# One batch's convolution moved from TensorE to VectorE, its buffers cut into four units, and a new order of work

## The chip, the cores and the metric

The kernel runs on one core of one Trainium2 chip. The time is the device time of one execution, in microseconds (us); a profiled execution also gives the span from its first to its last instruction. The engines are TensorE (PE in the profile; its weight loads are PEld), VectorE (DVE), ScalarE (ACT), GpSimd (POOL) and SyncE (SP). GpSimd issues nearly all loads, SyncE the stores and some transposes by DMA.

## The reference

An attention without softmax, whose normed result goes through a feed-forward layer with a gate made by a convolution over the sequence. B = 8 batches, H = 8 heads, S = 576 positions, D = 64; the model is 512 wide and the hidden layer 1024.

```python
kv = np.einsum('bhsd,bhse->bhde', k, v)
out = np.einsum('bhsd,bhde->bhse', q, kv)
rms = np.sqrt(np.mean(out * out, axis=-1, keepdims=True) + 1e-06)
attn = out / rms * g_norm
x = attn.transpose(0, 2, 1, 3).reshape(B, S, H * D)
h = np.maximum(x @ w_in, 0.0)
hp = pad(h, one position on either side)
conv_out = sum(conv_w[k][None, None, :] * hp[:, k:k + S, :] for k in range(3))
gate = 1.0 / (1.0 + np.exp(-conv_out))
return h * gate @ w_out
```

## The kernel before

The work is cut into small operations, each a Python function marked `@op`. A long string, `ORDER` (L67 to L121), lists them as tokens: `hm.1.7@4` calls `hm(1, 7)` and gives it PSUM bank 4 (or a slot of a ring of buffers), `:1` picks VectorE in place of ScalarE for a copy or a relu (for `qc` and `qc0` the other way round). The loop at L797 runs the tokens, and L807 to L815 chain the instructions of each engine in that order. So every engine runs its own instructions strictly in the order of the list, and the engines meet only where one needs the result, or the buffer, of another.

The steps of a batch b:

- `Lq`, `Lk`, `Lv` (L304 to L310) load q, k and v of a batch through POOL's queue, casting to bf16; each has a ring of two buffers. `Li` and `Lo` load quarters of w_in and halves of w_out. Batch 0 is loaded in pieces by `pre` (L217), batch 1 in halves.
- `kv` (L349) makes the k-v product of a batch on TensorE, `kvc`, `kvn` and `ky` copy it out of PSUM.
- `qt`, `qtp` (L404) turn q round on TensorE and `qc` copies it. For batches 5, 6 and 7 `dq` (L434) does it by a transposing DMA on SP's queue.
- `ot` or `oq` multiplies q with kv, `sq` squares the result. For batches 0 and 1 `on` sums the squares on TensorE, `nl` makes the root on ScalarE and `mu0` the normed x on VectorE. For later batches `oc` copies the result out, `ss` sums the squares, `ln` and `sl` make the factors, `sp` spreads them and `mu` multiplies; batch 7 takes its factors through DRAM (`fw`, `fr`).
- `hm(b, f)` (L634) is one eighth f of the hidden layer: 8 matmuls of 288 columns. `re` is its relu from PSUM into `h`. Batch 1's first two are split into `ha` and `hb`.
- The convolution works on pairs j of eighths. `CONV` groups the batches: group 0 is batch 0, group 1 batch 1, groups 2, 3 and 4 are two batches each. `ta` (L694) writes the two outer taps times h, `aa` (L704) adds them shifted, `ab` adds h, all on VectorE; `sg` (L736) is the sigmoid on ScalarE, which works in the same buffer; `mg` (L748) multiplies h by it on VectorE. In place of `ta`, `aa` and `ab`, `cm(c, f)` (L724) makes the convolution as 6 matmuls with diagonal weights (built by `dg`), and `sg` reads PSUM. The kernel before does that for eighths 6 and 7 of batches 0 and 1.
- `om` (L756) multiplies 128 rows of h by w_out, `ea` copies the result to a row buffer, and `st` stores it through SP. Pairs of batches 0 and 3 (`SPLIT`) take the eight parts in two halves.
- `unread` issues matmuls on a constant whose result nobody reads ("fills").

The convolution's buffers are two tiles, `taps[0]` and `taps[1]` (L198), each for two batches. A group of one batch takes a whole one and uses half of it.

Of the kernel before, what the change touches and what calls it, by code (L numbers as in the profile page):

```python
# [67 lines left out]
pre@0,0,0 unread.10@0 qt0.0.0@0 ps pn pi ca.k.0 ca.v.0 kv.0.0.1@1 kvc.0.0.1.0:1@0 ct@2 qt0.0.1@3 qc0.0.0:1@0
kvc.0.0.1.1 ot.0.0@0 qc0.0.1:1 unread.3@4 kv.0.1.1@3 Lq.1.0@1 pg sq.0.0@0 on.0.0@4 al.x0@0 al.h1@0 nl.0.0@0 pc
dg.7:1 kvc.0.1.1.0:1 dg.6:1 unread.1@6 qt0.0.2@2 kvc.0.1.1.1:1 ot.0.1@6 unread.3@3 kv.0.2.1@3 sq.0.1@1 mu0.0.0  # L70
al.x1@1 Li.1 al.h0@1 kvc.0.2.1.0:1 Li.3 qc0.0.2:1@1 kvc.0.2.1.1:1 on.0.1@4 nl.0.1@1 qt0.0.3@2 Lv.1.0@1 ot.0.2@0
mu0.0.1 sq.0.2@2 qc0.0.3:1 unread.3@3 kv.0.3.1@4,5 kvc.0.3.1.0 on.0.2@6 kvc.0.3.1.1:1 nl.0.2@2 ot.0.3@4 mu0.0.2
sqh.0.3.0@3 unread.3@3 onh.0.3.0@6 sqh.0.3.1 onh.0.3.1 nlh.0.3.0@3 muh.0.3.0 Lk.1.0@1 qt.1.0@0 nlh.0.3.1 qc.1.0:1@2
muh.0.3.1 Li.0 hm.0.2@6 re.0.2 ta.0.2@0 hm.0.3@4 re.0.3 hm.0.6@6 Lq.1.2 ta.0.3 Lv.1.2 re.0.6 aa.0.1 hm.0.7@4 Lk.1.2
Lq.2.0@0 cm.0.6@6 re.0.7:1 sg.0.6@1 kv.1.0.2@0 cm.0.7@4 kvc.1.0.2.0:1@1 kvc.1.0.2.1 sg.0.7 ot.1.0@0 hm.0.1@6 ab.0.1
sq.1.0@4 re.0.1 qt.1.1@4 hm.0.0@2 on.1.0@6 mg.0.3 qc.1.1@3 ot.1.1@4 nl.1.0@4 re.0.0:1 sq.1.1@5 kv.1.2.2@2
kvc.1.2.2.0 ta.0.0@1 mu0.1.0 kvc.1.2.2.1 on.1.1@6 Li.2 ot.1.2@2 nl.1.1@5 ot.1.3@0 ta.0.1 sq.1.2@6 mu0.1.1 aa.0.0
unread.1@6 on.1.2@6 sq.1.3@7 ab.0.0 nl.1.2@6 mu0.1.2 on.1.3@4 nl.1.3@7 Lk.2.0@0 qt.2.0@6 sg.0.3 qt.2.1@4 mu0.1.3
ha.1.2@2 hb.1.2 qc.2.1@4 sg.0.2 qc.2.0@0 ha.1.3@0 hb.1.3 re.1.2 re.1.3 hm.1.7@4 Lv.2.0@0 hm.0.4@2 mg.0.1 Lq.3.0@1
hm.0.5@0 sg.0.1 Lk.3.0@1 Lv.3.0@1 re.1.7 sg.0.0 pl ta.1.2@0 re.0.4 ta.1.3 re.0.5 hm.1.4@4 kv.2.0.4@2 Lo.0 aa.1.1  # L80
ab.1.1 mg.0.0 sg.1.3 sg.1.2 kvc.2.0.4.0@0 hm.1.5@0 kvc.2.0.4.1 ta.0.4@1 ta.0.5 ot.2.0@2 mg.1.1 aa.0.2 hm.1.6@6
re.1.4 ot.2.2@4 re.1.5 sq.2.0@0 ta.1.4@0 ab.0.2 re.1.6 qt.3.1@0 oc.2.0:1@0 qt.3.0@6 qc.3.1@1 hm.1.1@2 ot.2.1@0
sq.2.2@1 sg.0.4 oc.2.2@1 sg.0.5 sq.2.1@2 Lo.1 Lq.4.0@0 Lq.5.0@1 qc.3.0@2 ta.1.5 ot.2.3@4 re.1.1:1 sq.2.3@3 hm.1.0@6
oc.2.1 Lk.4.0@0 Lv.4.0@0 kv.3.0.4@2 re.1.0 ss.2@3 oc.2.3 mg.0.2 ln.8@0 aa.1.2 kvc.3.0.4.0:1@1 kvc.3.0.4.1:1 ab.1.2
unread.3@0 ot.3.0@4 ta.1.0@1 ot.3.1@6 sq.3.0@4 ot.3.2@0 ta.1.1 al.x2@0 oc.3.0@2 aa.1.0 sq.3.2@5 oc.3.2@3 sq.3.1@6
om.0.3.0@2 om.0.0.0@3 oc.3.1 sl.8@0 om.0.1.0@4 ot.3.3@0 om.0.1.4 ab.1.0 om.0.3.4 sq.3.3@7 oc.3.3 sp.2.1@6,0 ss.3@5
dq.5.0@3 ea.0.1@0 mu.2.1.0 Lk.5.0@1 mu.2.1.1 om.0.0.4 ea.0.3@1 ln.1@0 sp.2.0@4,6 mu.2.0.1 mu.2.0.0 dq.5.1@0
om.0.2.0@2 Lv.5.0@1 sg.1.5 sg.1.4 qtp.4.0@0 cm.1.6@6 qc.4.0@4 mg.1.2 ea.0.0@2 hm.2.5@4 sl.1@0 hm.2.2@0 sg.1.1
om.0.2.4 re.2.5 sg.1.6@0 re.2.2 ea.0.2@3 sg.1.0 sp.3.0@6,4 cm.1.7@0 mu.3.0.1 mu.3.0.0 hm.2.4@2 hm.2.7@6 sg.1.7
sp.3.1@0,4 mg.1.0 re.2.4 mg.1.3 kv.4.0.4@2 mu.3.1.0 mu.3.1.1 re.2.7 kvn.4.0.4 ky.4.0.4.0 ky.4.0.4.1 qtp.4.1@6  # L90
hm.3.4@0 hm.3.5@4 re.3.4 oq.4.1@0 re.3.5 qc.4.1@2 ta.2.4@1 ta.2.5 oq.4.0@2 hm.2.6@6 sq.4.0@0 hm.3.3@4 oc.4.0@1
hm.3.6@2 sq.4.1@1 re.2.6 aa.2.2 Lq.7.0@0 hm.3.7@6 re.3.3 oc.4.1 hm.3.1@0 re.3.6 re.3.7 hm.3.2@6 hm.2.3@2 om.0.6.0@4
st.0.0 ab.2.2 ta.2.6@0 sg.2.5 re.3.1 re.3.2 ta.2.7 oq.4.3@6 oq.4.2@0 sg.2.4 re.2.3 kv.5.0.4@5 sq.4.2@2 Lv.7.0@0
Lk.7.0@0 om.0.6.4 om.0.5.0@2 aa.2.3 ab.2.3 Lk.6.0@1 Lv.6.0@1 kvn.5.0.4 sq.4.3@3 oc.4.2@0 mg.2.2 ky.5.0.4.0:1
ea.0.6@4 ss.4@3 dq.7.0@1 oc.4.3 ky.5.0.4.1:1 oq.5.0@0 oq.5.1@4 sq.5.0@4 ta.2.2@1 om.0.5.4 sq.5.1@5 oc.5.0:1@2
om.0.4.0@6 oc.5.1 ta.2.3 oq.5.3@0 oq.5.2@4 aa.2.1 om.0.8.0@7 ea.0.5@5 ab.2.1 sq.5.3@6 om.0.4.4 sq.5.2@7 ss.5 ln.2@0
om.0.8.4 hm.2.1@2 oc.5.2@3 ea.0.8@6 oc.5.3 re.2.1 sl.2@0 hm.2.0@4 sp.4.1@0,2 ea.0.4@7 om.0.7.0@7 re.2.0 mu.4.1.0
mu.4.1.1 sp.4.0@4,0 kv.7.0.4@6 mu.4.0.0 sg.2.2 mu.4.0.1 om.0.7.4 kvn.7.0.4:1 sg.2.3 ea.0.7@2 sp.5.0@4,2 hm.3.0@0
al.h2@1 re.3.0 kx.7.0.4.0 dq.7.1@4 mu.5.0.1 mu.5.0.0 hm.4.5@2 re.4.5 sp.5.1@6,4 hm.4.1@0 mg.2.1 mu.5.1.0 hm.4.2@2
mu.5.1.1 ta.2.0@1 sg.2.7 hm.4.0@6 hm.5.3@4 ta.2.1 re.4.1 sg.2.6 mg.2.3 kx.7.0.4.1 re.4.0 re.4.2 oq.7.0@0 re.5.3  # L100
kv.6.0.4@6 oq.7.1@4 sq.7.0@0 hm.5.2@2 oc.7.0@1 aa.2.0 Lq.6.0@1 hm.4.3@0 st.0.4 dq.6.0@2 sq.7.1@1 oc.7.1 re.5.2
hm.4.4@4 st.0.5 kvn.6.0.4:1 ab.2.0 ta.3.2@0 re.4.3 hm.5.6@0 st.0.1 ta.3.3 hm.5.4@2 hm.5.1@6 sg.2.1 sg.2.0 re.4.4
re.5.6 re.5.1 re.5.4 hm.5.0@4 oq.7.3@6 oq.7.2@0 aa.3.1 re.5.0 mg.2.0 om.1.6.0@2 om.1.3.0@3 ab.3.1 st.0.3 kx.6.0.4.0
st.0.6 ta.3.0@1 dq.6.1@3 sq.7.3@2 sq.7.2@3 ta.3.1 sg.3.3 sg.3.2 hm.5.5@4 oc.7.2@0 st.0.7 aa.3.0 ss.7@0 mg.3.1 ln.4@0
al.x3@1 ab.3.0 ta.3.4@0 ea.1.3@7 re.5.5 om.1.1.0@1 oc.7.3 ea.1.6@5 kx.6.0.4.1 om.1.0.0@0 fw.4 fr.7.0@0 ea.1.1@0
oq.6.0@2 oq.6.2@6 oq.6.3@4 om.1.8.0@1 ta.3.5 ea.1.0@1 sq.6.2@4 fr.7.1@1 oc.6.2@2 oq.6.1@6 aa.3.2 om.1.4.0@0 sq.6.0@5
sq.6.3@6 sq.6.1@7 oc.6.0@3 ss.6@2 ab.3.2 oc.6.1 ea.1.8@4 ln.3@0 ea.1.4@2 hm.4.6@6 om.1.5.0@2 oc.6.3 sl.3@0 st.1.0
mu.7.0.0 sp.6.0@4,0 mu.7.0.1 re.4.6 sg.3.5 sg.3.4 ea.1.5@1 mu.6.0.0 mu.6.0.1 om.1.2.0@6 hm.4.7@4 hm.5.7@0 mu.7.1.0
om.1.7.0@7 re.4.7 sg.3.1 re.5.7 st.0.8 sp.6.1@4,2 st.0.2 st.1.8 mg.3.2 mu.7.1.1 al.h3@0 ta.3.6@0 ea.1.2@6 ea.1.7@3
hm.7.6@0 ta.3.7 sg.3.0 hm.7.2@6 re.7.6 re.7.2 mu.6.1.0 mu.6.1.1 aa.3.3 mg.3.0 ab.3.3 hm.6.0@4 re.6.0 hm.7.1@0  # L110
hm.7.0@4 re.7.1 re.7.0 st.1.2 hm.6.1@0 hm.7.3@4 hm.6.2@6 hm.7.5@2 re.6.1 ta.4.0@1 st.1.1 st.1.7 sg.3.6 sg.3.7 ta.4.1
re.7.3 re.6.2 re.7.5 hm.6.6@0 hm.6.3@4 re.6.6 re.6.3 hm.6.7@2 aa.4.0 mg.3.3 ab.4.0 hm.6.4@4 hm.7.4@0 ta.4.2@0 re.6.7
sg.4.1 sg.4.0 ta.4.3 aa.4.1 om.2.5.0@2 hm.6.5@6 mg.4.0 re.7.4 re.6.4 re.6.5 om.2.7.0@3 hm.7.7@6 ea.2.5@4 ab.4.1
sg.4.2 sg.4.3 re.7.7 ea.2.7@6 ta.4.4@1 om.2.1.0@2 om.2.4.0@6 ta.4.5 aa.4.2 mg.4.1 ab.4.2 ta.4.6@0 ta.4.7 om.3.6.0@3
om.2.2.0@7 ea.2.1@0 st.2.7 st.2.1 aa.4.3 om.2.3.0@2 om.2.8.0@4 om.2.6.0@5 st.1.3 ea.2.4@3 om.3.3.0@6 st.1.5 ab.4.3
om.2.0.0@0 sg.4.4 sg.4.5 ea.2.2@6 ea.2.3@0 sg.4.7 sg.4.6 mg.4.2 mg.4.3 om.3.3.4 ea.2.8@7 ea.2.6@1 om.3.1.0@2
om.3.6.4 st.1.6 om.3.4.0@7 st.2.8 om.3.1.4 om.3.4.4 ea.2.0@5 ea.3.3@7 st.2.2 om.3.2.0@6 oh.3.8.0@0 om.3.5.0@5
# [7 lines left out]
def kernel(  # L125
# [567 lines left out]
    @op  # L693
    def ta(c, f):  # L694
        h, n = span(c)
        if f % 2 == 0:
# [2 lines left out]
        nc.vector.tensor_scalar_mul(tap[:, 0, f % 2, :n, 8:8 + S], h[:, f], cwn[:, 0, f:f + 1])  # L699
        nc.vector.tensor_scalar_mul(tap[:, 1, f % 2, :n, :S], h[:, f], cwn[:, 2, f:f + 1])  # L700
# [145 lines left out]
```

## Time and profile before

| | |
|---|---|
| median of 3 runs | 179.97 us (179.6 to 180.15) |
| span of the profiled execution | 177.6 us |
| `hm` matmuls (L640) | 496 recorded, 64.5 us |
| `om` matmuls (L761) | 268 recorded, 63.0 us |
| `cm` matmuls (L731) | 24, 5.4 us |
| relu on ScalarE (L646) | 61, 37.9 us |
| row copies on ScalarE (L341, 512 wide) | 35, 20.6 us |

A group's line of the profile names the line of code, engine, operation, the tile written and the tiles read, the shape, and a count; then the busy time, the mean of one in ns, and how long its engine sat idle just before such instructions, and for what. Instructions of one engine overlap a little, so the step from start to start is shorter than the mean of one. L341 and L343 are the helper `copy`, and serve many operations.

The chain is read in order of time: start, length, and what the time was spent on. The landing of a load is counted from its issue.

### The profile page before, as it was taken

Reading aid. Unit: us, or ns where it says so; the run is one execution under the profiler, and the core shown is the slowest. Engines: PE = TensorE matmul, PEld = TensorE weight load, DVE = VectorE, ACT = ScalarE, POOL = GpSimd, SP = SyncE. Lnnn points to the kernel's source line nnn. Section 1 sums busy time; section 2 is a strip of 40 time slices with the busy share of each in tenths; the row PEclk is TensorE's granted clock in tenths of the full one; section 3 lists DMA queues with packets and bytes.
Section 4 is the critical chain, followed back from the end, with each engine's and each line's share of the span. In section 5 each row is a group of like instructions: output and inputs, shape, how many; then the busy total and the mean of one; then the engine's idle time right before and its main releaser. Section 6 shows DMA issues by size and latency. Waiting matters only on the chain.

```text
span 177.6 us, 4060 instructions
## 1 busy us (share of the span) xinstructions
PE 168.4 (95%) x1641; PEld 101.3 (57%) x1660; DVE 139.5 (79%) x235; ACT 149.7 (84%) x233; POOL 30.8 (17%) x54
## 2 busy tenths in 40 slices
...
GB/s 155 188 183 197 200 204 201 205 203 206 205 204 203 198 192 139 174 203 198 160 201 179 293 128 0 53 219 263 21 160 0 4 0 143 152 82 99 258 352 219
DMA packets 36219, 29.49 MB, mean 166 GB/s; under 512 B 8528, under 2 KB 31720, under 8 KB 36200
## 3 DMA queue, kind: packets, MB, share of 16 engines
...
q8 instruction: 13, 0.21, 0.4%
...
q10 hardware_dynamic: 40, 0.01, 0.0%
...
## 4 chain that ended last, share of the span: by engine, by line
PE 70%; DMA 20%; POOL 4%; ACT 2%; issue 2%; POOLq 0%; ACTq 0%
PE bank L761 33%; PE bank L640 27%; DMA v_sb<-in_v_dram 10%; DMA k_sb<-in_k_dram 7%; DMA q_sb<-in_q_dram 4%; PE bank L358 3%; PE bank L464 2%; POOL q_sb L241 1%; PE bank L603 1%; PE bank L575 1%; POOL v_sb L241 1%; POOL k_sb L241 1%; PE bank L776 1%; PE bank L731 1%; PE bank L388 1%
## 5 line engine op out<-in xcount | busy, mean ns | idle before, releaser
L640 PE MATMUL bank<-xT,w_in_sb 128*128 128x288 bf16 x496 | 64.5, 286 | 0.1
L761 PE MATMUL bank<-w_out_sb,h 128*128 128x512 bf16 x268 | 63.0, 379 | 1.1 <-issue 0.6
L640 PEld LDWEIGHTS <-w_in_sb 128*128 128x128 bf16 x496 | 47.6, 98 | 14.1 <-issue 0.5
L761 PEld LDWEIGHTS <-h 128*128 128x128 bf16 x280 | 26.3, 98 | 30.6 <-issue 1.9
L646 ACT ACTIVATE h<-bank 128x576 bf16<-128x576 f32 x61 | 37.9, 657 | 4.2 <-PE bank L640 3.9
L745 ACT ACTIVATE taps<-taps,cwn 128x1152 bf16<-128x1152 bf16 (+1 forms) x36 | 38.2, 1094 | 0.1
L341 ACT ACTIVATE row<-bank 128x512 f32<-128x512 f32 (+1 forms) x37 | 21.3, 598 | 12.3 <-PE bank L761 9.3
L751 DVE TENSOR_TENSOR h<-h,taps 128x2304 bf16<-128x2304 bf16 (+1 forms) x20 | 22.2, 1113 | 2.0 <-ACT taps L745 1.2
L706 DVE TENSOR_TENSOR taps<-taps 128x2304 bf16<-128x2304 bf16 (+1 forms) x18 | 20.9, 1160 | 0.4
L712 DVE TENSOR_TENSOR taps<-taps,h 128x2304 bf16<-128x2304 bf16 (+1 forms) x18 | 20.8, 1153 | 0.3
L699 DVE TENSOR_SCALAR taps<-h,cwn 128x1152 bf16<-128x1152 bf16 (+1 forms) x36 | 16.7, 463 | 2.5 <-ACT h L646 2.4
L493 ACT ACTIVATE sq<-bank 128x576 bf16<-128x576 f32 x28 | 17.9, 676 | 0.0
L700 DVE TENSOR_SCALAR taps<-h,cwn 128x1152 bf16<-128x1152 bf16 (+1 forms) x36 | 17.5, 487 | 0.0
L629 DVE SCALAR_TENSOR_TENSOR xT<-o,cw,bank 128x576 bf16<-128x576 f32 x20 | 15.3, 809 | 2.7 <-PE bank L603 2.5
L341 ACT ACTIVATE o<-bank 128x576 f32<-128x576 f32 x22 | 15.0, 694 | 0.0
...
L427 PE MATMUL bank<-fill 128*128 128x512 bf16 x25 | 9.0, 480 | 1.7 <-DVE fill L228 1.5
L358 PEld LDWEIGHTS <-k_sb 96*64 96x64 bf16 x384 | 7.3, 114 | 4.0 <-issue 2.6
L358 PE MATMUL bank<-v_sb,k_sb 96*64 96x64 bf16 x384 | 8.5, 199 | 1.0 <-DMA k_sb<-in_k_dram 0.7
L301 POOL DMA_DIRECT2D k_sb<-in_k_dram x8 | 6.1, 758 | 14.4 <-PE bank L358 12.5
L562 DVE SCALAR_TENSOR_TENSOR xT<-bank,cw,root 128x576 bf16<-128x576 f32 x7 | 5.6, 815 | 1.8 <-ACT root L542 1.7
...
## 6 DMA issues: line engine op xcount, KB each, us to landing
...
q_sb<-in_q_dram POOLq DMA_DIRECT2D x6, 576.0 KB, 13.7
k_sb<-in_k_dram POOLq DMA_DIRECT2D x6, 576.0 KB, 14.7
v_sb<-in_v_dram POOLq DMA_DIRECT2D x6, 576.0 KB, 16.3
...
```

The costliest lines, as they stand in the source:

```text
L341: nc.scalar.activation(to, fr, AX.Copy)
L358: nc.tensor.matmul(ps[i][i * D:(i + 1) * D, t - t0, :], k_sb[:, 2 * t + i, r * D:(r + 1) * D], v_sb[:, 2 * t + i, r * D:(r + 1) * D], star ...
L493: nc.scalar.activation(in_order(b, s), product(b, t), AX.Square)
L640: nc.tensor.matmul(ps[:, e, :HS], w_in_sb[:, t, f * P:(f + 1) * P], x[:, t, e * HS:(e + 1) * HS], start=(t == 0), stop=(t == NT - 1))
L646: nc.scalar.activation(to, fr, AX.Relu)
L699: nc.vector.tensor_scalar_mul(tap[:, 0, f % 2, :n, 8:8 + S], h[:, f], cwn[:, 0, f:f + 1])
L700: nc.vector.tensor_scalar_mul(tap[:, 1, f % 2, :n, :S], h[:, f], cwn[:, 2, f:f + 1])
L706: nc.vector.tensor_add(tap[:, 1, :, :n, :S], tap[:, 0, :, :n, 7:7 + S], tap[:, 1, :, :n, 1:1 + S])
L712: nc.vector.tensor_add(y, y, h[:, 2 * j:2 * j + 2])
L745: nc.scalar.activation(y, y, AX.Sigmoid, scale=cwn[:, 1, f:f + 1])
L751: nc.vector.tensor_mul(h, h, T["tap", c, j][:, 1, :, :n, :S])
L761: nc.tensor.matmul(T["om", p, m], h[:, f, m * P:(m + 1) * P], w_out_sb[:, f, :], start=(f == 0), stop=(f == NF - 1))
```

## The change

Three things. Batch 1's eighths 6 and 7 go the way of the others: `cm.1.6` and `cm.1.7` are gone, `ta.1.6`, `ta.1.7`, `aa.1.3` and `ab.1.3` are new. The two `taps` tiles become one tile of four one-batch units; a new helper `units(n)` takes one or two of them, and a group of one batch now takes one unit. And `ORDER` is replaced throughout: another sequence, other banks and slots, other choices between ScalarE and VectorE, another order of the loads on POOL, of the transposes and stores on SP, and four fills fewer. Behind `pi` the line numbers of the new kernel are 2 higher.

```diff
+    def units(n):
+        s = slots.pop(0)
+        return taps[:, s:s + n].rearrange("p b k f w -> p k f b w")
...
-    taps = [consts.tile([P, 2, 2, 2, TW], BF16, name=f"taps{i}") for i in range(2)]
+    taps = consts.tile([P, 4, 2, 2, TW], BF16, name="taps")
...
-        for t in taps:
-            nc.vector.memset(t[:, 0, :, :, 7:8], 0.0)
-            nc.vector.memset(t[:, 1, :, :, S:S + 1], 0.0)
+        nc.vector.memset(taps[:, :, 0, :, 7:8], 0.0)
+        nc.vector.memset(taps[:, :, 1, :, S:S + 1], 0.0)
...
     def ta(c, f):
...
-            T["tap", c, f // 2] = taps[slots.pop(0)]
+            T["tap", c, f // 2] = units(CONV[c][1])
...
     def sg(c, f):
...
-                T["tap", c, f // 2] = taps[slots.pop(0)]
+                T["tap", c, f // 2] = units(CONV[c][1])
```

Of the order, the stretch from batch 1's last kv to batch 3's kv, before:

```
kv.1.2.2@2
kvc.1.2.2.0 ta.0.0@1 mu0.1.0 kvc.1.2.2.1 on.1.1@6 Li.2 ot.1.2@2 nl.1.1@5 ot.1.3@0 ta.0.1 sq.1.2@6 mu0.1.1 aa.0.0
unread.1@6 on.1.2@6 sq.1.3@7 ab.0.0 nl.1.2@6 mu0.1.2 on.1.3@4 nl.1.3@7 Lk.2.0@0 qt.2.0@6 sg.0.3 qt.2.1@4 mu0.1.3
ha.1.2@2 hb.1.2 qc.2.1@4 sg.0.2 qc.2.0@0 ha.1.3@0 hb.1.3 re.1.2 re.1.3 hm.1.7@4 Lv.2.0@0 hm.0.4@2 mg.0.1 Lq.3.0@1
hm.0.5@0 sg.0.1 Lk.3.0@1 Lv.3.0@1 re.1.7 sg.0.0 pl ta.1.2@0 re.0.4 ta.1.3 re.0.5 hm.1.4@4 kv.2.0.4@2 Lo.0 aa.1.1
...
```

and after:

```
kv.1.2.2@4
ab.0.1 on.1.1@6 kvc.1.2.2.0 kvc.1.2.2.1 ot.1.2@4 nl.1.1@1 ot.1.3@0 mu0.1.1 sq.1.2@0 on.1.2@6 Lq.2.0@0 sq.1.3@1
ta.0.0@2 on.1.3@2 nl.1.2@0 ta.0.1 mu0.1.2 nl.1.3@1 sg.0.2 mu0.1.3 aa.0.0 ab.0.0 ha.1.2@6 ha.1.3@2 mg.0.3 hb.1.2 hb.1.3
re.1.2 ta.1.2@3 hm.0.4@0 kv.2.0.4@4 re.1.3 ta.1.3 qt.2.0@2 sg.0.3 sg.0.0 qt.2.1@6 re.0.4 hm.0.5@0 mg.0.1 aa.1.1 sg.0.1
ta.0.4@0 ab.1.1 mg.0.0 kvc.2.0.4.0@0 kvc.2.0.4.1 sg.1.3 re.0.5 qc.2.1@0 hm.1.6@4 ot.2.2@6 sg.1.2 re.1.6 sq.2.2@0
...
```

The loads on POOL behind batch 0's, in the order of issue (i2 is a quarter of w_in, o0 a half of w_out, q1a a half of batch 1):

```
before: q1a i1 i3 v1a k1a i0 q1b v1b k1b q2 i2 k2 v2 q3 k3 v3 o0 o1 q4 q5 k4 v4 k5 v5 q7 v7 k7 k6 v6 q6
after:  q1a i1 i3 k1a v1a q1b i0 v1b k1b v2 i2 k2 q2 q3 v3 k3 o0 o1 v4 q4 q5 k4 k5 v5 v6 v7 k6 k7 q7 q6
```

The transposes on SP: before `dq.5.0 dq.5.1 dq.7.0 dq.7.1 dq.6.0 dq.6.1`, after `dq.5.1 dq.5.0 dq.7.0 dq.6.1 dq.7.1 dq.6.0`. The two `kx.7` copies, which stood before and behind `dq.7.1`, now follow `dq.6.1`. `st.1.1` moves from among the first stores of its pair to the last stores of the kernel.

More of the change, by code (lines that the diff above doesn't have):

```diff
@@ L67 @@
 ORDER = """
[L68 to L117, printed above, removed]
@@ L118 @@
-om.3.0.0@4 st.2.3 ea.3.6@6 ea.3.1@0 st.3.6 st.3.3 st.3.1 st.2.4 st.2.5 om.3.5.4 om.3.2.4 om.3.7.0@2 st.2.6 ea.3.4@6
-st.2.0 eh.3.8.0@7 st.3.4 om.3.0.4 ea.3.5@0 om.3.7.4 oh.3.8.1 ea.3.2@3 ea.3.0@4 ea.3.7@1 st.3.5 st.1.4 sh.3.8.0
-st.3.2 st.3.0 st.3.7 eh.3.8.1 sh.3.8.1
+pre@0,0,0 al.x0@0 unread.10@6 qt0.0.0@0 pi ct@1 ca.v.0 ca.k.0 qt0.0.1@2 kv.0.0.1@3 kvc.0.0.1.0:1@0 Lq.1.0@1
+qc0.0.0:1@0 kvc.0.0.1.1:1 pg unread.2@6 ot.0.0@4 dg.6:1 kv.0.1.1@3 kvc.0.1.1.1:1 kvc.0.1.1.0:1 sq.0.0@0 Li.1 al.h1@0
+unread.2@6 on.0.0@0 qc0.0.1:1 ot.0.1@6 nl.0.0@0 qt0.0.2@2 pc mu0.0.0 sq.0.1@0 qc0.0.2@0 unread.2@3 kv.0.2.1@3
@@ new lines @@
+kvc.0.2.1.0 on.0.1@0 kvc.0.2.1.1:1 Li.3 nl.0.1@0 Lk.1.0@1 mu0.0.1 unread.1@5 qt0.0.3@4 Lv.1.0@1 ot.0.2@2 sq.0.2@0
+qc0.0.3 unread.3@1 kv.0.3.1@5,0 al.h0@1 kvc.0.3.1.1 Lq.1.2 kvc.0.3.1.0:1 on.0.2@6 ps Li.0 ot.0.3@4 Lv.1.2 nl.0.2@0
+sqh.0.3.0@0 unread.3@0 onh.0.3.0@0 pn sqh.0.3.1 Lk.1.2 mu0.0.2 nlh.0.3.0@1 muh.0.3.0 onh.0.3.1 nlh.0.3.1 qt.1.0@6
+muh.0.3.1 qc.1.0:1@0 Lv.2.0@0 hm.0.2@2 hm.0.6@0 dg.7:1 hm.0.7@4 Li.2 re.0.6 cm.0.6@6 re.0.2 kv.1.0.2@0 sg.0.6@0
+kvc.1.0.2.0@0 kvc.1.0.2.1 re.0.7:1 Lk.2.0@0 hm.0.3@2 cm.0.7@4 ta.0.2@1 ot.1.0@0 qt.1.1@6 sg.0.7 re.0.3:1 sq.1.0@0
```

40 lines of the change are left out of this document (added).

## The prediction

> **What bounds the kernel now.** I read the page first (busy shares, then the chain that ended last), then the busy time by stage, then the chain in order of time, and last where single loads land.
>
> ```profile
> span 177.6 us, 4060 instructions
> PE 168.4 (95%) x1641; PEld 101.3 (57%) x1660; DVE 139.5 (79%) x235; ACT 149.7 (84%) x233; POOL 30.8 (17%) x54
> PE 70%; DMA 20%; POOL 4%; ACT 2%; issue 2%; POOLq 0%; ACTq 0%
> ```
>
> 70% of the chain is TensorE work, and the DMA fifth is loads of q, k and v that TensorE waits for early on. The stages, cut at TensorE's waits, the fifth a part of the fourth (columns: stretch, length, then busy us of PE, PEld, DVE, ACT, POOL, the granted clock, DMA share, GB/s):
>
> ```profile
> 0.00:27.00 27.00, 23.99 (x271) 13.77 (x274) 17.30 (x57) 18.81 (x30) 17.25 (x29) 1.00 1.20 188
> 27.00:36.60 9.60, 8.36 (x120) 6.10 (x121) 9.24 (x18) 9.27 (x16) 4.81 (x14) 1.00 1.33 202
> 36.60:45.90 9.30, 8.90 (x147) 6.46 (x147) 9.18 (x19) 9.26 (x18) 2.38 (x3) 1.00 1.30 205
> 45.90:158.90 113.00, 111.92 (x1030) 67.48 (x1042) 103.73 (x145) 106.27 (x161) 6.38 (x8) 1.00 0.78 143
> 63.90:118.50 54.60, 53.97 (x603) 33.05 (x605) 49.89 (x67) 53.26 (x85) 4.74 (x6) 1.00 1.00 162
> 158.90:177.60 18.70, 15.25 (x78) 7.51 (x77) 0.00 (x0) 6.12 (x11) 0.00 (x0) 1.00 0.65 239
> ```
>
> Until 46 us the DMA engines never rest (about 200 GB/s in every stretch), so a load's landing is set by how many bytes stand ahead of it in POOL's queue, not by when it is issued. From 45.9 TensorE is busy 111.92 of 113 us: there the order of its own work is the time, with ScalarE (106.27) and VectorE (103.73) close behind. The clock is 1.00 throughout. Two pieces of the chain and two landings carry the sum below:
>
> ```profile
> 28.67 17.11 DMA v_sb<-in_v_dram
> 45.91 0.95 PE bank L358 x48
> 47.22 0.32 PE bank L427
> 47.59 0.38 PE bank L427
> 57.05 0.74 PE bank L731 x6
> 60.85 0.85 PE bank L731 x6
> ```
>
> The first two lines: batch 3's v lands at 45.78 and its kv follows at once. The next two are three fill matmuls (an `unread.3`) on the chain. The last two are the convolution matmuls `cm.1.6` and `cm.1.7`.
>
> ```profile
> q_sb<-in_q_dram POOLq DMA_DIRECT2D x1, 576.0 KB, 12.5
> v_sb<-in_v_dram POOLq DMA_DIRECT2D x1, 576.0 KB, 15.6
> ```
>
> These are batch 2's q (issued at 17.07, landed 29.6) and v (issued at 21.03, landed 36.6), the first and the last of the group q, w_in quarter, k, v.
>
> **The change part by part.**
>
> *Off TensorE.* `cm.1.6` and `cm.1.7` go: 0.74 + 0.85 = 1.59 us of the chain. The `unread.3` at 47.2 goes: 0.32 + 0.38 = 0.70. Before 27 us there are 23 fills in both orders, and the single one at 29.0 stood in a wait of the norms: nothing. Gain: 2.29 us, all of it after 36.6.
>
> *Onto VectorE.* `ta.1.6`, `ta.1.7`, `aa.1.3`, `ab.1.3` from these rows (mean ns of one):
>
> ```profile
> L700 DVE TENSOR_SCALAR taps<-h,cwn 128x576 bf16<-128x576 bf16 x12 | 4.8, 398 | 0.0
> L706 DVE TENSOR_TENSOR taps<-taps 128x1152 bf16<-128x1152 bf16 x6 | 4.5, 757 | 0.1
> L712 DVE TENSOR_TENSOR taps<-taps,h 128x1152 bf16<-128x1152 bf16 x6 | 4.5, 753 | 0.1
> L699 DVE TENSOR_SCALAR taps<-h,cwn 128x576 bf16<-128x576 bf16 x12 | 4.4, 364 | 1.6 <-ACT h L646 1.6
> ```
>
> 2 x (0.364 + 0.398) + 0.757 + 0.753 = 3.0 us. The two sigmoids read the buffer (L745, 0.78) and no longer PSUM (L742, 0.65): +0.3 us for ScalarE. The new order also turns engines over: 10 more relus net and 13 output copies go from ScalarE to VectorE, at about 0.66 and 0.61 us from start to start. Added up over the order, ScalarE loses about 9.6 us and VectorE gains about 16.4, of which 1.7 come before 45.9, 3.6 after the last convolution product, and 11.1 between.
>
> *The order of the loads.* Batch 2 was q, w_in, k, v and becomes v, w_in, k, q: the same bytes, so the last place lands at 36.6 as before, but it is now q's. TensorE's list: `kv.1.2.2` (its k lands at 27.0 in both), the norms of batch 1, `ha`/`hb`, `hm.0.4`, `kv.2.0.4`, then `qt.2.0`, which needs that q. The norms end as before (the `mu0.1.3` product at about 32.1, one product earlier in VectorE's list), `hb.1.3` at 32.9, `hm.0.4` 0.98 (L640, 16 matmuls in 1.96), kv 0.88: TensorE stands at 34.7 and q comes at 36.6, a wait of 1.9. `hm.0.5`, which could fill it, is behind `qt.2.0` in the list. Nothing overtakes on TensorE, and what is queued behind (all of batch 1's remaining `hm`) is late with it. Measured as work: by 36.6 the kernel before has done 1.27 (`qt.2`) and 2.57 of `hm` where the new one has done 0.98 + 0.88. It is 1.98 us behind. Bounds: 0 if q lands by 34.7, which the queue's 2.9 us per load (590 KB at 200 GB/s) excludes unless v, w_in or k is smaller; 2.5 if its semaphore is late.
>
> So of 2.29 us saved, 1.98 are spent at 36.6: -0.3.
>
> *The transposes of batch 5.* `dq.5.0` was issued at 56.4 and `dq.5.1` at 58.3, landing 10.7 and 16.0 us later, against running loads. Now q of batch 5 is the third load after w_out (the old order was q4, q5, k4, v4, the new one is v4, q4, q5, k4): it lands at 59.2 instead of 56.3, `dq.5.1` goes first and `dq.5.0`, which `oq.5.0` needs, second: 59.3 + 1.9 + 16.0 = 77.2. TensorE's work up to `oq.5.0` puts it there at 76.7 (no wait in between) to 77.3 (at the 5% that the kernel before lost between kv of batch 2 and `oq.5.0`). Cost 0 to 1.0; I take 0.3.
>
> *The last loads.* v6, v7, k6, k7, q7, q6: the queue was full to 95.1 in the kernel before, now `dq.7` stands behind it; k7 comes fourth and lands at about 85.7 to 86.5, and `kv.7.0.4` stands at 85.4. Cost 0 to 1; I take 0.3. `kx.7` is issued on SP behind `dq.6.1`, which waits for q6 (91.5): it lands at 96, `oq.7.1` wants it at 96.8, so it is hidden by 0.8.
>
> *The stores* wait longer (`st.1.1` now almost at the end, SP issuing one each 0.6 us): about 0.2 after TensorE's end.
>
> *The four units.* One tile for two. With two batches an add now walks 2x2x576 in three steps where it walked 4x576. No row shows that form. Nearest rows: with gaps after each 576 (L706, two batches) 1.362 us against 1.352 without (L751): a step costs about 0.01. I take 0; the other end, VectorE's rate for 576 elements from PSUM (0.754 us, over twice as slow per element), would add about 1.2 us to each of 24 adds. [...]
>
> *VectorE's room.* From 45.9 to its last product (158.9) it was busy 103.73 of 113.0. With 11.1 more it needs 114.8. The first matmul that needs the last product (`om.3.2.4`) stands 10.4 us of work before TensorE's end (about 173.9 by the terms above): at about 163.4. That leaves 117.5 us, so VectorE may idle 2.7 us where it idled 9.3 (2.93 of it in one wait for ln.3 at 119). ScalarE, the tight one before, idled 1.3 of 54.6 us between 63.9 and 118.5 without TensorE waiting, so 2% can be held; I charge 0.6 of the possible 6.6.
>
> **The sum** against the profiled span: -2.29 + 1.98 + 0.3 + 0.3 + 0.2 + 0.6 = +1.1, with terms that partly hide each other (a TensorE that is late at `oq.5.0` finds k7 landed): I count 0.3 to 0.5 of overlap and take +0.7, span 178.3. The runs stand 2.4 above the span (179.97 against 177.6): **180.7 us**, 0.4% slower. The forecast's own range is 179.7 to 181.7.
>
> **Rivals.**
>
> *The gain is kept (faster).* It is one place: the wait at `qt.2.0`. For it: only this wait takes the gain back before 60 us, and ScalarE, tight before, is 9.6 us lighter. Against it: the full queue. From q landing before 35.9 (0.7 earlier) on, the kernel is no slower; with no wait there and the others absorbed it is -2.29 + 0.2, some 178 us. With half of it, 179.2.
>
> *VectorE becomes the bound.* Its idle time stays at half of the old (4.7, not 2.7): +2.0 on top of -0.3 + 0.2, and the last products come late: 182; at the whole 9.3, 186. For it: every stage from 46 on is planned within 2% of full. Against it: the idle was slack in a kernel in which nothing waited for VectorE.
>
> [...]
>
> *Nothing in it matters:* the terms cancel within measurement.
>
> **Chances.** Forecast (saved work spent on waiting, +0.2 to +1.7) 0.46; cancelled to within 0.54 us either way, 0.2; gain kept, 0.21; VectorE the bound, 0.11; adds slower, 0.02. About 0.3%, 0.54 us, is what a measurement of this kernel tells from no change. A tenth of the forecast's case falls within it: same 0.25. Faster is the kept gain, 0.21. Slower is the rest of the forecast, VectorE and the adds: 0.54. The range reaches from the half-kept gain to VectorE's lower price with something over: 179.0 to 183.0.
>
> **What would show it.** Right: TensorE idle for 1 to 2 us at about 35 us before the transposes of q (L382), released by q's DMA; kv of batch 3 still at about 45.9 behind its load; VectorE busy over 97% from 46 to the last product; adds of 2304 still 1.35 us. Wrong: TensorE without that wait (the gain is kept), a last product after 164 us (VectorE the bound), adds above 1.4 us, or TensorE waits of over 2 us behind `dq.5.0` or k7.

## The result and the profile after

| | median, us | range, runs | ratio to before, 95% interval |
|---|---|---|---|
| before | 179.78 | 179.54 to 180.15, 4 | |
| the changed kernel | 182.78 | 180.69 to 183.48, 4 | 1.0139 [1.0093, 1.0185] |
| the changed kernel, a second time | 181.59 | 180.20 to 183.52, 12 | 1.0088 [1.0050, 1.0127] |

The change is slower, by 0.9 to 1.4%, and its runs spread over 3 us. (The ratios leave disturbed runs out; the medians are over all runs.) The profiled execution took 182.47 us with a span of 180.7, 3.1 above the span of before. Its page:

```profile
span 180.7 us, 4054 instructions
PE 165.3 (91%) x1628; PEld 100.0 (55%) x1644; DVE 155.1 (86%) x259; ACT 139.8 (77%) x213; POOL 30.9 (17%) x54
PE 56%; DMA 23%; DVE 7%; POOL 6%; ACT 3%; issue 3%; SPq 0%; POOLq 0%; ACTq 0%; DVEq 0%
```

TensorE has less to do (165.3 us recorded for 168.4) and VectorE 15.6 more, as the order said. But TensorE's share of the last chain fell from 70 to 56%, and DMA, VectorE and GpSimd took it: TensorE now waits. The timeline of TensorE says where (start, length, line and shape; in brackets the idle time just before and what ended it):

```profile
37.40 1.21 PE L382 MATMUL bank<-ident,q_sb 96*64 96x96 bf16 x48 [1.62 <-DMA q_sb<-in_q_dram]
63.45 0.95 PE L360 MATMUL bank<-v_sb,k_sb 96*64 96x64 bf16 x48 [0.33 <-DVE xT L631]
78.19 0.31 PE L466 MATMUL bank<-qT,kvn 64*64 64x288 bf16 x1 [0.60 <-DMA qT<-q_sb]
89.39 0.95 PE L360 MATMUL bank<-v_sb,k_sb 96*64 96x64 bf16 x48 [2.09 <-DMA k_sb<-in_k_dram]
106.90 0.31 PE L466 MATMUL bank<-qT,kvx 64*64 64x288 bf16 x1 [0.46 <-DMA kvx<-kvn]
```

They are `qt.2.0`, `kv.4`, `oq.5.0`, `kv.7` and `oq.6.0`. The five waits are 1.62 + 0.33 + 0.60 + 2.09 + 0.46 = 5.10 us. Before, TensorE had none above 0.3 after 30 us. The 2.29 us of work that left TensorE taken off, 2.81 us of delay should be seen at its last matmul; it ends at 177.00 for 174.25, 2.75 later. So these waits are the loss; after 107 us there is no further one. The fit is closer than the method is good for. A sixth wait of 0.32 us at 33.03, for batch 1's normed x, is not in the sum. `b_units` below has the matmuls of the kernel before, and its last one ends 0.56 later (174.81). And in a second profile of the changed kernel the same sum gives 1.70 where the end is 0.94 later. Read it as good to about 0.8 us.

Four of the five end with a DMA, and the largest is `kv.7` for batch 7's k. The chain in order of time leads from it back to its cause (start, us, what):

```profile
72.92 0.90 PE bank L360 x48
73.82 0.28 issue
74.11 0.77 POOL v_sb L303
74.88 0.03 POOL k_sb L303
74.91 0.97 issue
75.88 13.46 DMA k_sb<-in_k_dram
89.35 0.04 issue
89.39 0.95 PE bank L360 x48
```

`kv.5` ends at 73.8 and frees slot 1 of the k and v rings (each ring has two buffers, slots 0 and 1). Only then can GpSimd issue `Lv.7`, and behind it `Lk.6` and `Lk.7`; k7 then needs 13.46 us, and `kv.7` starts 0.04 us after it has landed. GpSimd's own timeline shows what stood in its queue meanwhile:

```profile
64.71 0.77 POOL L303 DMA_DIRECT2D v_sb<-in_v_dram  x1 [12.74 <-PE bank L360]
74.11 0.77 POOL L303 DMA_DIRECT2D v_sb<-in_v_dram  x1 [8.62 <-PE bank L360]
74.87 1.78 POOL L303 DMA_DIRECT2D k_sb<-in_k_dram  x2
```

For 8.62 us after `Lv.6` it issues nothing. `Lk.6`, whose buffer `kv.4` had freed at 64.4, waits with the rest. The kernel before had such a pause too, of 9.11 us, but v7 and k7 went out ahead of it (the second and third line):

```profile
65.74 0.77 POOL L301 DMA_DIRECT2D q_sb<-in_q_dram  x1 [16.55 <-PE bank L388]
66.50 0.77 POOL L301 DMA_DIRECT2D v_sb<-in_v_dram  x1
67.26 0.77 POOL L301 DMA_DIRECT2D k_sb<-in_k_dram  x1
77.14 0.77 POOL L301 DMA_DIRECT2D k_sb<-in_k_dram  x1 [9.11 <-PE bank L358]
```

The stages of 70 to 75 us, after and then before (length, busy PE, PEld, DVE, ACT, POOL, granted clock, DMA share, GB/s):

```profile
70.00:72.50 2.50, 2.50 (x26) 1.69 (x25) 2.46 (x3) 2.50 (x5) 0.00 (x0) 1.00 1.34 53
72.50:75.00 2.50, 2.34 (x59) 1.66 (x58) 2.50 (x5) 2.49 (x5) 0.89 (x2) 1.00 1.57 109
```

```profile
70.00:72.50 2.50, 2.50 (x23) 1.98 (x22) 2.46 (x4) 2.50 (x6) 0.00 (x0) 1.00 1.44 112
72.50:75.00 2.50, 2.45 (x21) 1.84 (x20) 2.46 (x4) 2.50 (x4) 0.00 (x0) 1.00 1.12 212
```

The last column falls to 53 and 109 GB/s where before it was 112 and 212. Only v6 is on its way, beside the transposes of batch 5.

Two other things asked of the profile. The adds on the four-unit buffer keep their time (1362 and 1354 ns before):

```profile
L708 DVE TENSOR_TENSOR taps<-taps 128x2304 bf16<-128x2304 bf16 x12 | 16.3, 1359 | 0.2
L714 DVE TENSOR_TENSOR taps<-taps,h 128x2304 bf16<-128x2304 bf16 x12 | 16.3, 1354 | 0.2
```

And VectorE from 46 us to near its last product (which ends at 166.5) is busy 111.27 of 116.5 us, 95.5%:

```profile
46.00:162.50 116.50, 112.04 (x1073) 68.10 (x1082) 111.27 (x161) 100.84 (x151) 8.06 (x10) 1.00 0.76 134
```

### The profile page after: what moved, and what is told of

Same layout as the page of the kernel before. It is cut to its first block, busy times and chain, and to the rows that moved or that the text cites. A ratio compares the mean times of both kernels' runs of the same rounds, so it can differ in the third digit from the quotient of the medians.

```text
span 180.7 us, 4054 instructions
## 1 busy us (share of the span) xinstructions
PE 165.3 (91%) x1628; PEld 100.0 (55%) x1644; DVE 155.1 (86%) x259; ACT 139.8 (77%) x213; POOL 30.9 (17%) x54
## 4 chain that ended last, share of the span: by engine, by line
PE 56%; DMA 23%; DVE 7%; POOL 6%; ACT 3%; issue 3%; SPq 0%; POOLq 0%; ACTq 0%; DVEq 0%
PE bank L763 26%; PE bank L642 23%; DMA q_sb<-in_q_dram 9%; DMA k_sb<-in_k_dram 7%; DMA v_sb<-in_v_dram 5%; DVE xT L631 3%; PE bank L360 3%; DMA kvx<-kvn 2%; POOL q_sb L244 1%; POOL v_sb L244 1%; DVE taps L708 1%; PE bank L466 1%; POOL k_sb L244 1%; PE bank L778 1%; PE bank L382 1%
## 5 line engine op out<-in xcount | busy, mean ns | idle before, releaser
L642 PE MATMUL bank<-xT,w_in_sb 128*128 128x288 bf16 x496 | 65.3, 286 | 0.6 <-DMA w_in_sb<-in_moe_w_in_dram 0.5
L747 ACT ACTIVATE taps<-taps,cwn 128x1152 bf16<-128x1152 bf16 (+1 forms) x38 | 39.9, 1079 | 6.2 <-DVE taps L714 6.2
L648 ACT ACTIVATE h<-bank 128x576 bf16<-128x576 f32 x51 | 32.3, 657 | 8.0 <-PE bank L642 7.8
L343 ACT ACTIVATE row<-bank 128x512 f32<-128x512 f32 (+1 forms) x24 | 13.4, 591 | 11.6 <-PE bank L778 6.2
L714 DVE TENSOR_TENSOR taps<-taps,h 128x2304 bf16<-128x2304 bf16 (+1 forms) x19 | 21.5, 1133 | 0.3
L701 DVE TENSOR_SCALAR taps<-h,cwn 128x1152 bf16<-128x1152 bf16 (+1 forms) x38 | 17.9, 471 | 0.1
L702 DVE TENSOR_SCALAR taps<-h,cwn 128x1152 bf16<-128x1152 bf16 (+1 forms) x38 | 17.6, 464 | 0.0
L631 DVE SCALAR_TENSOR_TENSOR xT<-o,cw,bank 128x576 bf16<-128x576 f32 x20 | 15.3, 811 | 2.7 <-PE bank L605 2.4
L650 DVE TENSOR_SCALAR h<-bank 128x576 bf16<-128x576 f32 x13 | 9.8, 753 | 4.6 <-PE bank L642 4.6
L345 DVE COPY row<-bank 128x512 f32<-128x512 f32 x13 | 8.8, 686 | 5.6 <-PE bank L763 3.5
L343 ACT ACTIVATE o<-bank 128x576 f32<-128x576 f32 x20 | 13.0, 669 | 0.0
L303 POOL DMA_DIRECT2D v_sb<-in_v_dram x8 | 6.0, 756 | 31.0 <-PE bank L360 28.9
## 6 DMA issues: line engine op xcount, KB each, us to landing
v_sb<-in_v_dram POOLq DMA_DIRECT2D x6, 576.0 KB, 15.6
```

The source lines that it names most:

```text
L343: nc.scalar.activation(to, fr, AX.Copy)
L631: nc.vector.scalar_tensor_tensor(x_tile(b)[:, 2 * u:2 * u + 2, n], T["o32", b, u][:, :, n], g_sb, T["sp", b, e][u][:, :, :HS], op0=AL.mult ...
L642: nc.tensor.matmul(ps[:, e, :HS], w_in_sb[:, t, f * P:(f + 1) * P], x[:, t, e * HS:(e + 1) * HS], start=(t == 0), stop=(t == NT - 1))
L648: nc.scalar.activation(to, fr, AX.Relu)
L714: nc.vector.tensor_add(y, y, h[:, 2 * j:2 * j + 2])
L747: nc.scalar.activation(y, y, AX.Sigmoid, scale=cwn[:, 1, f:f + 1])
```

## The experiments

They ran in three groups, each beside runs of the kernel before on the same chip: its median was 180.12 in the first group (31 runs), 180.22 in the second (25) and 179.62 in the third (29). "Waits" are TensorE's in the profiled execution.

**First group: one part alone or undone**

`b_units`: the four-unit buffer alone, in the kernel before, with its own order.

```diff
+    def units(n):
+        s = slots.pop(0)
+        return taps[:, s:s + n].rearrange("p b k f w -> p k f b w")
...
-            T["tap", c, f // 2] = taps[slots.pop(0)]
+            T["tap", c, f // 2] = units(CONV[c][1])
```

> The kernel before with its own order, but the one tile of four units in place of two tiles: the layout alone. Theory (the layout costs nothing): adds of 2304 stay at 1.35 us and the time is that of the kernel before within 0.3 us. Rival (three-step walks are slower): adds above 1.4 us and the time 0.5 us or more longer.

Measured: 179.82 us (179.06 to 180.71, 10 runs), ratio 0.9990 [0.9956, 1.0023]. The buffer's form costs nothing.

`b_conv`: `b_units`, and batch 1's eighths 6 and 7 on VectorE.

```diff
- qtp.4.0@0 cm.1.6@6 qc.4.0@4 ... sg.1.6@0 ... cm.1.7@0 mu.3.0.1
+ qtp.4.0@0 qc.4.0@4 ... sg.1.6 ... mu.3.0.1
- ab.1.0 om.0.3.4
+ ab.1.0 ta.1.6@1 ta.1.7 aa.1.3 ab.1.3 om.0.3.4
```

> The kernel before with its own order, four units, and batch 1's eighths 6 and 7 on VectorE (ta.1.6, ta.1.7, aa.1.3, ab.1.3 behind ab.1.0; cm.1.6 and cm.1.7 gone): the named change without the new order. Theory (the new order lost the time, not the convolution): TensorE's list is 1.59 us shorter, VectorE takes 3.0 us more at 52 to 56 us, where it idled 1.0, so mu of batches 2 and 3 come up to 2 us later and give part of it back; the time is 0 to 1.2 us below the kernel before. Rival (VectorE's load is what slowed the kernel): 0.5 to 2 us above the kernel before.

Measured: 181.07 us (180.31 to 183.91, 10 runs), ratio 1.0074 [1.0042, 1.0107]. The rival's number: slower, although TensorE has 1.59 us less to do. Its waits from 46 us on (engine, line, what it waited for: us in all, times, longest):

```profile
PE bank L605 <- DVE xT L631: 0.8, 1, 0.8
PE bank L642 <- DVE xT L631: 0.6, 2, 0.4
PE bank L642 <- ACT row L343: 0.4, 1, 0.4
```

VectorE's 3 us stand ahead of the normed products of batches 2 and 3 (L631), for which TensorE waits. With nothing else changed, these waits come to 1.8 us. They are not the whole delay: `kv.4` starts 19.20 us after `kv.3` where in `b_units` it starts 18.23 after it, 0.97 later with some 1.5 us of matmuls taken out in between, so about 2.5 us are lost there. From `kv.4` to the last matmul's end both take 110.39.

`a_hm`: the changed kernel with `re.0.4 hm.0.5@0` ahead of `qt.2.0@2`, to fill the wait for batch 2's q.

> The changed kernel with re.0.4 and hm.0.5 ahead of qt.2.0, so that one eighth of the hidden layer stands in the wait for batch 2's q. Theory (TensorE idle at 35.8 to 37.4 is lost time): the wait of 1.62 us shrinks to about 0.6 and the time falls by about 1.0. Rival (ScalarE and VectorE, busy over 97% there, would have held TensorE up later anyway): the wait shrinks, kv of batch 3 still starts at 46.5, the time moves by less than 0.3.

Measured: 181.91 us (180.09 to 182.53, 10 runs), ratio 1.0082 [1.0046, 1.0118]. The wait at `qt.2.0` is gone; 0.89 us came back at 39.9, where the matmul behind it waits for the copy of q. At `kv.7` TensorE still waited 2.22 us: k7 is issued only behind `kv.5`, and from `kv.5` to `kv.7` pass 16.0 us here, 16.5 and 15.9 in the two profiles of the changed kernel. No gain that can be told from the second measurement of the changed kernel (1.0088).

`a_k7`: the changed kernel with batch 7's k and v in the slot that comes free first.

```diff
- Lv.6.0@0 ... Lv.7.0@1 ... Lk.6.0@0 ... Lk.7.0@1
+ Lv.7.0@0 ... Lk.7.0@0 ... Lv.6.0@1 ... Lk.6.0@1
```

> The changed kernel, but batch 7 takes k/v buffer 0 (freed by batch 4's kv at 64.3) and batch 6 buffer 1 (freed by batch 5's kv at 73.8), and POOL loads v7, k7, v6, k6 in place of v6, v7, k6, k7. Theory (the place in POOL's queue): k7 was fourth behind v5 and is now second, so it lands about 83.5 in place of 89.35; the 2.09 us wait of TensorE before batch 7's kv goes, and the time falls by 1.5 to 2.1 us against the changed kernel. Rival (VectorE sets the end after 46 us and TensorE's wait there is slack): the wait goes, the time moves by less than 0.5 us.

Measured: 183.05 us (180.32 to 184.73, 10 runs), ratio 1.0088 [1.0045, 1.0131]. A miss, and an instructive one. Its waits from 60 us on:

```profile
PE bank L466 <- DMA kvx<-kvn: 2.5, 1, 2.5
PE bank L466 <- DMA qT<-q_sb: 1.3, 1, 1.3
```

The wait at `kv.7` is gone, but `oq.7` now waits 2.5 us for batch 7's small moves `kx.7`. They stand on SP behind the transposes `dq.7.0` and `dq.6.1`, which wait for their q and hold SP from 92.7 to 97.1; the moves are issued at 97.14 and take 3.87 us. In the changed kernel the late k7 had hidden this. The second line is `oq.5.0`, whose transpose took 17.18 us in this profile.

**Second group: the wait followed to its end**

`a_k7b`: `a_k7`, and `dq.6.1` behind `kx.7.0.4.0`.

```diff
- dq.6.1@0 kv.7.0.4@3 ... kx.7.0.4.1 ... kx.7.0.4.0
+ kv.7.0.4@3 ... kx.7.0.4.1 ... kx.7.0.4.0 dq.6.1@0
```

> The changed kernel with batch 7's k and v in slot 0 and batch 6's in slot 1, as in a_k7, and in addition dq.6.1 behind kx.7.0.4.0, so that batch 7's four small moves do not stand on SP's queue behind a transposition that waits for batch 6's q. Theory (the k7 load is the mis-sized term, 2.1 us, and a_k7 only exchanged it for a wait of 2.5 us for kx.7 behind that transposition): no wait over 0.5 us at kv.7 and none at oq.7, 180.3 to 181.3. Rival (the delay comes from VectorE's added work and shows wherever a load no longer hides it): the waits go, others on VectorE's products of batches 4 and 5 take their place, 182 to 183.

Measured: 179.82 us (178.72 to 180.58, 10 runs), ratio 0.9972 [0.9929, 1.0014]. It is better than expected, and the whole loss is gone, with the convolution still on VectorE. GpSimd's issues:

```profile
63.74 0.77 POOL L303 DMA_DIRECT2D v_sb<-in_v_dram  x1 [12.83 <-PE bank L360]
64.50 0.77 POOL L303 DMA_DIRECT2D k_sb<-in_k_dram  x1
73.14 0.77 POOL L303 DMA_DIRECT2D v_sb<-in_v_dram  x1 [7.86 <-PE bank L360]
```

v7 and k7 go out at 64 us, where `Lk.7` had gone out at 75.9, and `kv.7` starts at 86.16 with no wait. The rest is read from the waits after 30 us:

```profile
PE bank L382 <- DMA q_sb<-in_q_dram: 1.3, 1, 1.3
PE bank L466 <- DMA kvx<-kvn: 0.5, 1, 0.5
PE bank L466 <- DVE h L753: 0.5, 1, 0.5
PE bank L360 <- DVE xT L631: 0.3, 1, 0.3
```

1.28 + 0.51 + 0.50 + 0.33 = 2.62 us of waits against 2.29 us saved: +0.3, and TensorE ends at 174.35 for 174.25. So the waits that are left use up what was saved.

`a_best`: `a_k7b`, `a_hm`'s edit, `dq.5.0` ahead of `dq.5.1`, and the store `st.0.8` behind batch 6's small moves.

> a_k7b with the three other places mended as well: re.0.4 and hm.0.5 ahead of qt.2.0 (fills the wait for batch 2's q), dq.5.0 ahead of dq.5.1, and the store st.0.8 behind batch 6's small moves. The convolution stays all on VectorE. Theory (the whole loss is in the order of loads and transfers, the convolution on VectorE saves its 1.6 us of TensorE): all waits over 0.5 us after 30 us gone, 178.0 to 179.2, faster than before by 0.3 to 1 per cent. Rival (VectorE's work is the bound once the loads are in time): TensorE waits for VectorE's products (line 631) for 1 to 3 us in all, 180.5 to 182.

Measured: 180.35 us (178.36 to 182.54, 10 runs), ratio 0.9960 [0.9910, 1.0011]. Not told from no change; the time that the theory gave did not come. Of the waits 0.99 us at `oq.7` stayed, again for `kx.7`: `dq.7.0` stands ahead of it on SP and waits for q7 until 91.8.

`a_fill`: the changed kernel with `unread.8@3` ahead of `kv.7.0.4@3`.

> The changed kernel with eight filler matmuls (128x512, about 0.22 us each, 1.75 us together) on TensorE just ahead of kv.7, so that the wait for batch 7's k load is filled and TensorE does not fall silent there. Theory (the runs with a mean granted clock near 0.991 are runs in which TensorE was silent for over 2 us ahead of kv.7 and was then granted half its clock for some 3.5 us, about 1.7 us lost): the load and the start of kv.7 stay as they are, no half clock is seen after kv.7, the highest of the runs comes down by 1.5 to 2 us and the median to about 181.0 to 181.8. Rival (the lowered clock comes by itself and has nothing to do with the wait): as many runs near clock 0.991 as with the changed kernel, median 182 to 183. Second rival (fillers in front of kv.7 cost time): kv.7 starts later by up to 1.75 us, median above 183.

Measured: 182.13 us (181.63 to 182.45, 4 runs), ratio 1.0103 [1.0039, 1.0166]. The fills close the gap (0.45 us are left) and `kv.7` starts at 89.53 for 89.39, so in this profile they do not delay it. The median lies in the first rival's 182 to 183 and not in the theory's range. The one run of the four with a lowered mean clock (0.991) was the fastest, 181.63; the three others, at 0.997 to 1.0, took 181.94 to 182.45, so here it is not the clock that keeps the time up. Four runs don't decide more; the clock is taken up at the end.

`b_conv2`: `b_conv` with VectorE's added work where it had idled before.

```diff
- ab.1.0 ta.1.6@1 ta.1.7 aa.1.3 ab.1.3
+ ab.1.0
...
- sl.1@0 ... sg.1.6 ... sg.1.7 ... mg.1.3 ... qc.4.1@2
+ sl.1@0 ta.1.6@1 ... qc.4.1@2 ta.1.7 aa.1.3 ab.1.3 ... sg.1.6 sg.1.7 ... mg.1.3
```

> The kernel before with the four-unit buffer and batch 1's last two feature tiles on VectorE, as b_conv, but their work placed where VectorE idled (ta.1.6 ahead of mu.3, the rest behind qc.4.1 at about 66 us, the activations and mg.1.3 there too) and not ahead of batch 2's products; loads in the order of before. Theory (b_conv lost its gain to 1.5 us of TensorE's waits for batch 2's and 3's products behind the 2.9 us of added VectorE work): those waits go, 178.2 to 179.0. Rival (3.7 us more work on VectorE and 1.5 us of ScalarE's that now comes later cost TensorE the same wherever they stand, next at batch 4's products): 180 to 181.5.

Measured: 181.18 us (180.90 to 182.30, 10 runs), ratio 1.0077 [1.0042, 1.0112]. A miss: the rival's number. The waits for the normed products shrink (0.5 us in two are left at L631), but the sigmoids now come late on ScalarE, the output copy of batch 4 behind them, and TensorE waits for that copy's bank:

```profile
70.39 4.88 PE L642 MATMUL bank<-xT,w_in_sb 128*128 128x288 bf16 x36 [1.25 <-ACT o L343]
```

**Third group: the other way round**

`b_late`: the kernel before, convolution and all, with only its last loads in the changed kernel's order.

```diff
- Lv.7.0@0 Lk.7.0@0 ... aa.2.3 ab.2.3 Lk.6.0@1 Lv.6.0@1
+ Lv.6.0@0 Lv.7.0@1 ... aa.2.3 ab.2.3 Lk.6.0@0 Lk.7.0@1
```

> The kernel before (convolution partly on TensorE, as it was) with only the late loads in the changed kernel's manner: batch 6's k and v in slot 0, batch 7's in slot 1, GpSimd's order v6, v7, k6, k7. Theory (the order of the last loads makes the loss): k7 is issued only after kv.5, near 75 us, and lands at 87 to 89; TensorE waits 1 to 2.5 us at kv.7 and perhaps for batch 7's small moves behind it; 181.0 to 182.5, ratio 1.006 to 1.014. Rival (the loss comes from VectorE's added work): within 0.3 per cent of before.

Measured: 187.63 us (187.32 to 188.84, 6 runs), ratio 1.0449 [1.0406, 1.0492]. The mechanism is confirmed with the convolution left as it was, and its size was underrated: 1 to 2.5 us of waiting were expected, 5.05 came. `Lv.7` gets slot 1 from `kv.5` only at 77.9 here, 3.8 us later than in the changed kernel, so k7's transfer starts at 79.5 and takes 14.57 us:

```profile
94.08 1.49 PE L357 MATMUL bank<-v_sb,k_sb 96*64 96x64 bf16 x48 [5.05 <-DMA k_sb<-in_k_dram]
```

The rest of the 8 us is told at the end, with the clock.

`a_k7bcm`: `a_k7b` with the two eighths back on TensorE. In it `cm.1.6` takes PSUM banks 2 and 3 while `om.0.2`'s sum still lies in bank 3 and overwrites it, so this kernel does not compute 128 rows of the output; every instruction of both is there. An order that keeps that sum may be slower, which this run leaves out.

```diff
- ta.1.6@1 ... ta.1.7 ... aa.1.3 ... ab.1.3 ... sg.1.7 ... sg.1.6
+ cm.1.6@2 ... sg.1.6@1 ... cm.1.7@0 ... sg.1.7
```

> a_k7b with batch 1's last two feature tiles back on TensorE (cm.1.6 and cm.1.7, 0.7 to 0.85 us each, through the same one-batch buffer), so that the orders stay and only the named change is undone. Theory (with the loads in time, VectorE's share is hidden and TensorE's 1.6 us are a real gain): 1.0 to 1.7 us slower than a_k7b, 180.9 to 181.5. Rival (what TensorE is spared it waits for elsewhere, so the named change is worth nothing even here): within 0.5 us of a_k7b, 179.4 to 180.3.

Measured: 179.73 us (179.44 to 181.62, 12 runs), ratio 1.0001 [0.9973, 1.0028], where `a_k7b` had 0.9972 [0.9929, 1.0014]. The rival's number: on TensorE or on VectorE, the convolution of these two eighths makes no difference that can be told, even with the loads in time. The two intervals together leave room for up to about 1.4 us in favour of VectorE, so a part of the theory's 1.0 to 1.7 us is not excluded. Where the 1.59 us goes was not found: the profiled execution of this kernel has a stretch at half clock, and its waits (1.90 at `qt.2.0`, 0.56 at `cm.1.7`) can't be set beside those of `a_k7b`.

`a_k7c`: `a_best` with `dq.7.0` also behind `kx.7.0.4.0`.

> a_best with dq.7.0 too behind batch 7's small moves, so that these do not stand behind a transposition that waits for batch 7's q on SP's queue. Theory: the 1.0 us wait at oq.7 goes, of the waits after 30 us some 1.5 us stay (batch 2's q and its copy, 0.3 for VectorE), 178.3 to 179.3, faster than before by 0.3 to 0.9 per cent, and less scattered than a_best. Rival (the waits move on: oq.7 then waits for batch 7's transposed q instead): 179.5 to 180.5.

Measured: 179.48 us (177.91 to 180.52, 12 runs), ratio 0.9979 [0.9939, 1.0019]. The wait at `oq.7` for `kx.7` is gone, 0.73 us at 103.6 for a transposed q came in its place, so a part of what was saved moved on, as the rival had it. No version beats the kernel before by more than can be measured.

`after_again`: the changed kernel once more.

> The changed kernel once more, on the same chip and against the same runs of before as the other three, so that its ratio and theirs can be set side by side, and for how its runs spread with the mean granted clock. Expected: ratio 1.009 to 1.018, runs between 180.7 and 183.5 us. By the theory that a half clock follows the wait at kv.7 in some runs, those with a mean clock of 0.985 to 0.992 stand 1 to 2 us above those at 0.997 to 1.0; by its rival they do not differ.

Measured: 181.59 us, ratio 1.0088 [1.0050, 1.0127]; its profile has the same waits (1.19, 0.33, 2.04, 0.43) but the one at `oq.5.0`. The ratio and the fastest run (180.20) fall just below what was expected. The five runs with a mean clock of 0.991 or less have a median of 182.85, the seven others 180.7: the theory's side.

## Why the prediction was right, and where its sizes were off

Forecast were 180.7 us and "slower". Measured were 182.78 and, the second time, 181.59. Both lie within 179.0 to 183.0, but the first only just, and outside the forecast's own 179.7 to 181.7. The direction and the first wait were right for the reasons given; one term was far too small. Step by step:

- *2.29 us off TensorE:* the sum of waits against this number meets TensorE's end within 0.1 us in the changed kernel and within 0.3 in `a_k7b`, but only within 0.8 in the second profile of the changed kernel.
- *The wait at `qt.2.0`, 1.9 us, released by q's DMA:* right: 1.62, and 1.19 the second time. The late semaphore of its upper bound, 2.5, was not seen: q landed at 37.36 and TensorE started 0.04 later. That all of it is lost time is not shown: when `a_hm` filled it, 0.89 came back behind it and the time hardly moved. `kv.3` started at 46.49 and 45.32, about where it was named, but no longer behind its load.
- *`dq.5.0`, 0.3 us:* 0.60, and none above 0.25 the second time. Right in place and within its bounds.
- *The last loads, 0.3 us:* the mis-sized term. "The queue was full to 95.1 in the kernel before ... k7 comes fourth and lands at about 85.7 to 86.5": it landed at 89.35, the cost was 2.09 and 2.04, twice the upper bound given. This is the step that failed. The estimate counted bytes in a full queue. But the queue was not full (53 and 109 GB/s from 70 to 75 us): `Lv.7` waited for `kv.5` to free slot 1, and k6 and k7 stood behind it for 8.62 us. Which slot a load takes was on the page of the order, and its freeing time in the trace of before; I read the place in the queue and not the buffer. `a_k7b` takes the term away, together with the small moves behind it (0.9972); `b_late` makes it alone (1.0449).
- *`kx.7` hidden by 0.8 us:* right as it ran, but only because k7 was late; with k7 in time it showed as 2.5 us (`a_k7`). `kx.6`, which the store `st.0.8` held up on SP, was not priced: 0.46.
- *VectorE's room, 0.6 us:* measured 0.33 at `kv.4`, the only wait above 0.25 after 37 us that VectorE ended. The share of over 97% did not come (95.5%); in `a_k7b`, where TensorE waits less, it is 96.9% from 46 to 160 us, so TensorE's waits held VectorE up too. The last product ended at 166.5, past the 164 that I had named as the mark of VectorE being the bound; the mark was wrong, since all is 2.75 us late by then and TensorE waits nowhere behind it.
- *The four units, 0:* right (`b_units`, 0.9990). In the changed kernel the adds took 1359 and 1354 ns where they had taken 1362 and 1354, so of the other end, about 1.2 us more for each, nothing came.
- *The stores, 0.2:* the span ends 3.7 us after TensorE's last matmul where it ended 3.35 after it: 0.35 more.
- *The overlap, 0.3 to 0.5:* none came. A TensorE that is late at `oq.5.0` does not find k7 landed, because k7 is issued only when TensorE's own `kv.5` has freed the slot: the load is late with it (16.5, 15.9 and, in `a_hm`, 16.0 us from `kv.5` to `kv.7`).
- *From the span to the time, 2.4:* in every run whose span is on record the time is 1.7 to 1.9 above it. So some 0.6 us of the 180.7 stood for nothing in the kernel.

Put together as measured, -2.29 + 1.62 + 0.60 + 2.09 + 0.46 + 0.33 + 0.35 = 3.2 us where the span grew by 3.1 and the forecast had 0.7. That 180.7 still came as near as it did is luck in part: the 0.6 of the last step covered some of what the last loads lacked. Two signs that the prediction had named for being wrong came, waits of over 2 us behind k7 (2.09, 2.04) and the last product after 164. The first pointed at the term that failed; the second said nothing about VectorE.

Of the rivals, the gain was not kept: `qt.2.0` took most of it as forecast. That nothing matters is excluded by both intervals, and no add got slower (1359 and 1354 ns). VectorE as the bound is not what the changed kernel shows, but it is what the named change does in the old order (`b_conv`: 1.8 us of waits, 1.4 of them for VectorE). The new order makes room for it earlier in VectorE's list (`a_k7b` keeps pace with the kernel before), and loses the time with the loads.
